# Shifting the upper words of float64 weights: shift and AND with a constant column instead of two shifts by scalars

## The chip, the cores and the metric

The kernel runs on one core of one Trainium2 chip. The metric is the device time of one execution in microseconds; the kernel before takes 724.04 us (median of 3 runs, 724.02 to 725.27).

## What is computed

Causal attention with a gate bias for 2 x 8 heads of 576 positions, then two feed-forward blocks on its 1152 rows of 512 numbers. The first mixes four experts, the second multiplies two projections. The change lies in the loading of the second block's weights, which arrive as float64.

```python
out = np.zeros((N, D), dtype=np.float32)
for e in range(E):                       # E = 4, D = 512, F = 1024
    h = np.maximum(x @ w1[e], 0.0)
    out += p[:, e:e + 1] * (h @ w2[e])
...
a = x @ w_a                              # 512 -> 1536, float64 weights
b = x @ w_b
return (a * b @ w_out).astype(np.float32)
```

## The kernel before

Every float32 product is three TensorE products of a high and a low part (`mm3`, line 281: high by high, high by low, low by high). A weight is therefore split when it has landed: ScalarE writes the high part `wh` (line 80 or 225), and GpSimd or VectorE writes the low part `wl` (line 81 or 227) as the weight minus `wh`.

Attention and the plain part of the first block come first. From about 200 us on the kernel is a stream of units, each a pair of 256 weight columns against all rows: `quadrants` (line 417) forms the first-layer products `psq` and `pst` by a scheme of seven block products whose sums VectorE makes (line 436), and second-layer units add a tile of 128 rows into `acc` (lines 335 and 1225). `ab_stage(m)`, m = 0 to 5, is one pair of the second block: products with `wa`, products with `wb`, their product split by VectorE into `h2h` and `h2l` (lines 1202, 80, 81), and products with `wo`.

The float64 weights come as pairs of 32-bit words, in loads of 512 KB, into three SBUF buffers named `raw` (line 155; the DMA, line 156, is issued by SP). `narrow` (line 159) makes a float32 from each pair: ScalarE takes the absolute value of the upper word read as a float (line 161), GpSimd clamps it (line 162), VectorE shifts it (line 166), VectorE ORs in the lower word shifted right by 29 (line 170), and VectorE ORs in the sign and top exponent bit of the upper word (line 174). Line 174 is the last to read `raw`. A unit has six such pieces of 128 x 512 numbers: two for `wa`, two for `wb` (tile `tp`, followed on GpSimd by the four sums of lines 189 to 192 and two splits of 128 x 1024) and two for `wo` (tile `t`, followed by a split of 128 x 512). Six units make 36 pieces, so 36 instructions of each of the lines 161, 162, 166, 170 and 174; they run from 424 to 683 us.

The order on each engine is not written out: the program is recorded in the order of `run` (line 1309), where `weight_step` (line 251) loads or splits one piece per 3 us of planned TensorE work, and a scheduler then orders each engine's instructions by its own estimate of their durations. An instruction whose estimate changes can therefore move others. Engines run their queues strictly in order and wait on semaphores.

Of the kernel before, what the change touches and what calls it, by code (L numbers as in the profile page):

```python
# [8 lines left out]
F32 = mybir.dt.float32  # L9
F32R = mybir.dt.float32r  # L10
BF16 = mybir.dt.bfloat16
I32 = mybir.dt.int32
AF = mybir.ActivationFunctionType
ALU = mybir.AluOpType
# [6 lines left out]
P = 128  # L21
# [38 lines left out]
def fused_kernel(ctx, tc, qk0, v0, qT, kT, v, s, dp, w1, w2, wa, wb, wo, out):  # L60
    nc = tc.nc

    const = ctx.enter_context(tc.tile_pool(name="const", bufs=1))
# [9 lines left out]
    pr = const.tile([P, NTT, E], F32, name="pr")  # L73
    den = const.tile([P, NTT], F32, name="den")
    ident = const.tile([P, P], F32, name="ident")

    ckD = dram.tile([3, len(GROUPS), H, S], F32, name="ckD")

# [4 lines left out]
    def open_pools(c, names):  # L83
        for name, bufs in names:
            pools[name] = c.enter_context(tc.tile_pool(name=name, bufs=bufs))
# [72 lines left out]

    def narrow(t, lo, hi):

        nc.scalar.activation(out=t.bitcast(F32), in_=hi.bitcast(F32), func=AF.Abs)  # L161
        nc.gpsimd.tensor_scalar(  # L162
            out=t.bitcast(F32), in0=t.bitcast(F32), scalar1=2.0**-15, scalar2=GMAX,
            op0=ALU.max, op1=ALU.min,
        )
        nc.vector.tensor_scalar(
            out=t, in0=t, scalar1=5, scalar2=2,
            op0=ALU.logical_shift_left, op1=ALU.logical_shift_right,
        )
        nc.vector.scalar_tensor_tensor(  # L170
            out=t, in0=lo, scalar=29, in1=t,
            op0=ALU.logical_shift_right, op1=ALU.bitwise_or,
        )
        nc.vector.scalar_tensor_tensor(  # L174
            out=t, in0=hi, scalar=-(1 << 30), in1=t,
            op0=ALU.bitwise_and, op1=ALU.bitwise_or,
        )
# [21 lines left out]
    def split_piece(r, key, form, wide, src, j):  # L199
        wh, wl = slabs[key]  # L200
        if form == "half" and wide:
            t = pools["cv"].tile([P, SL], I32, tag="t", name="t")
            narrow(t, r[:, :, 0], r[:, :, 1])
            split(wh[:, j, :], wl[:, j, :], t.bitcast(F32), nc.gpsimd)
        elif form == "half":
            split(wh, wl, r, nc.gpsimd)
        elif form == "pair" and wide:
            if j == 0:
                wides[key] = pools["cv"].tile([P, NC, 2 * P], I32, tag="tp", name="tp")
            t = wides[key]  # L210
            narrow(t[:, 2 * j : 2 * j + 2], r[:, :, :, 0], r[:, :, :, 1])
            if j:
                split_pair(key, t.bitcast(F32), nc.gpsimd)
        elif form == "pair":
            split_pair(key, r, nc.vector)
        else:
            nsplit[0] += 1
            lo_eng = nc.gpsimd if nsplit[0] % 2 or nsplit[0] <= NFIRST else nc.vector
            two = slice(2 * j, 2 * j + 2)
            if nsplit[0] <= NFIRST:  # L220
                nc.gpsimd.tensor_scalar(
                    out=wh[:, two, :], in0=r, scalar1=1.0, scalar2=1.0, op0=ALU.mult, op1=ALU.mult
                )
            else:
                nc.scalar.activation(out=wh[:, two, :], in_=r, func=AF.Copy)
            for m in (2 * j, 2 * j + 1):
                lo_eng.tensor_tensor(
                    out=wl[:, m, :], in0=r[:, m - 2 * j, :], in1=wh[:, m, :].bitcast(F32), op=ALU.subtract
                )
# [530 lines left out]
    for base in (0, -32, -64, -96):  # L760
        nc.gpsimd.affine_select(
            out=sel_, in_=sel_, pattern=[[-1, H]], compare_op=ALU.not_equal,
# [5 lines left out]
        out=causal[:, S - P :], in_=causal[:, S - P :], pattern=[[-1, P]], compare_op=ALU.is_ge, fill=MASKED,  # L768
# [6 lines left out]
        out=cum[:NS, :NT0], data0=ones[:NS, :NT0], data1=sc[:, :NT0], initial=0.0,  # L775
        op0=ALU.mult, op1=ALU.add,
    )
    in_order(nc.vector.tensor_scalar(
        out=cb, in0=cum[:NS, :NT0], scalar1=1.0, scalar2=1.0, op0=ALU.mult, op1=ALU.mult
    ))  # L780
    for lo_, eng in ((slice(32, NB), nc.vector), (slice(96, NS), nc.gpsimd)):
        in_order(eng.tensor_tensor(
            out=cb[lo_], in0=cum[lo_, :NT0], in1=cb[lo_].bitcast(F32), op=ALU.subtract
# [197 lines left out]
    def close_attention():  # L981
        actx.close()
        open_pools(ctx, [("h2", 2), ("raw", 3), ("q", 2), ("cv", 1)])
        pools["late"] = True
        late_ps.append(ctx.enter_context(tc.tile_pool(name="ps_m2", bufs=5, space=PSUM)))
        for part_ in ("h", "l"):
            tq[part_] = ctx.enter_context(tc.tile_pool(name="tq" + part_, bufs=1)).tile(
                [P, 3, 2, SL], F32R, name="tq" + part_
            )
# [336 lines left out]
    mixed.clear()  # L1326
    passed.clear()
    close_attention()
    run(after, False)

# [59 lines left out]
```

## Time and profile before

| what | value |
|---|---|
| median of 3 runs | 724.04 us |
| profiled execution | 725.65 us, span 723.90 us (1.75 us lie around the span) |
| TensorE busy | 98% of the span, granted clock 10 tenths of full speed throughout |
| VectorE, GpSimd, ScalarE busy | 71%, 55%, 45% |
| costliest group | line 281, 334 products each of `wh,h2h`, `wl,h2h` and `wh,h2l`, 392, 389 and 390 ns |

TensorE's products overlap in the trace, so its busy time says only that some product was under way. What an instruction of another engine costs is read from the stretch it lies in: here 424 to 683 us, where the float64 weights are converted.

### The profile page before, as it was taken

What the parts mean: (1) busy time and instruction counts of PE and PEld (TensorE: products, weight loads), DVE (VectorE), ACT (ScalarE), POOL (GpSimd) and SP (SyncE); (2) the same over time, 40 slices, a digit from 0 to 9 for tenths busy, and PEclk for the clock granted to TensorE, in tenths of its full rate; (3) what the DMA queues carried; (4) which work ended last, traced back from release to release, by engine and by line L of the source; (5) the groups of instructions that cost most, each with busy time, mean ns of one, the idle gap of its engine ahead of it and who ended that gap; (6) DMA issues with size and microseconds to landing.
All of it is one profiled execution on the core that took longest, in us unless ns stands there. A gap on an engine that the chain in (4) does not pass through costs nothing.

```text
span 723.9 us, 10979 instructions
## 1 busy us (share of the span) xinstructions
PE 710.9 (98%) x3884; PEld 620.9 (86%) x3886; DVE 512.9 (71%) x1060; ACT 323.5 (45%) x722; POOL 398.8 (55%) x329
## 2 busy tenths in 40 slices
PE   9999999999999999999999999999999999999998
PEld 5886798999899888888888888887999888888886
DVE  5586878767686866765655666589973969787674
ACT  3597899877434333331223123334544424243410
POOL 5476866655235544430333057687277879788600
PEclk9999999999999999999999999999999999999999
DMA  8665434442111211120111021222021222212003
GB/s 328 209 176 141 126 88 119 124 120 62 57 41 58 89 58 58 59 65 24 58 59 47 13 88 59 88 87 88 30 87 59 88 88 83 92 60 88 1 0 131
DMA packets 33724, 61.42 MB, mean 85 GB/s; under 512 B 3285, under 2 KB 17525, under 8 KB 33669
## 3 DMA queue, kind: packets, MB, share of 16 engines
q1 hardware_dynamic: 33189, 59.61, 26.6%
q10 hardware_dynamic: 480, 1.11, 0.4%
q8 instruction: 31, 0.51, 0.3%
q14 instruction: 24, 0.20, 0.1%
HBM read 55.11 MB, written 2.58 MB: 80 GB/s over the span
## 4 chain that ended last, share of the span: by engine, by line
PE 76%; DVE 9%; POOL 5%; issue 4%; ACT 4%; DMA 3%; SPq 0%; POOLq 0%; ACTq 0%; DVEq 0%
PE ps L281 34%; PE psq L281 24%; PE pst L281 6%; PE av L702 2%; PE tr L670 2%; POOL wl L81 2%; PE ps L1037 2%; DMA raw<-in_wo 1%; DVE el L686 1%; DVE tp L174 1%; PE lullps L736 1%; ACT e L651 1%; DVE h2l L81 1%; DVE tp L170 1%; POOL tp L162 1%
## 5 line engine op out<-in xcount | busy, mean ns | idle before, releaser
L281 PE MATMUL ps<-wh,h2h 128*128 128x512 f32 (+1 forms) x334 | 131.1, 392 | 0.6 <-ACT h2h L80 0.6
L281 PE MATMUL ps<-wl,h2h 128*128 128x512 f32 (+1 forms) x334 | 129.9, 389 | 0.0
L81 POOL TENSOR_TENSOR wl<-raw,wh 128x1024 fp32r<-128x1024 f32 x24 | 58.2, 2433 | 129.0 <-ACT wh L80 98.6
L281 PE MATMUL ps<-wh,h2l 128*128 128x512 f32 (+1 forms) x334 | 125.6, 390 | 0.0
L335 DVE SCALAR_TENSOR_TENSOR acc<-ps,pr,acc 128x512 f32<-128x512 f32 x111 | 82.3, 746 | 41.1 <-PE ps L281 40.4
L281 PE MATMUL psq<-xh,wh 128*128 128x448 f32 (+1 forms) x224 | 81.7, 365 | 0.1
L281 PE MATMUL psq<-xh,wl 128*128 128x448 f32 (+1 forms) x224 | 81.4, 363 | 0.0
L281 PE MATMUL psq<-xl,wh 128*128 128x448 f32 (+1 forms) x224 | 81.3, 363 | 0.0
L281 PEld LDWEIGHTS ps<-wh,h2l 128*128 128x128 f32 x334 | 62.7, 188 | 13.2
L281 PEld LDWEIGHTS ps<-wh,h2h 128*128 128x128 f32 x334 | 62.8, 188 | 13.0 <-ACT h2h L80 1.3
L346 ACT ACTIVATE h2h<-psq 128x448 fp32r<-128x448 f32 (+1 forms) x56 | 29.5, 530 | 95.5 <-PE psq L281 76.4
L281 PEld LDWEIGHTS ps<-wl,h2h 128*128 128x128 f32 x334 | 62.8, 188 | 10.9
L81 POOL TENSOR_TENSOR wl<-sums,wh 128x1024 fp32r<-128x1024 f32 x24 | 58.3, 2427 | 4.9 <-ACT wh L80 4.9
L80 ACT ACTIVATE wh<-raw 128x1024 fp32r<-128x1024 f32 x24 | 25.5, 1062 | 69.6 <-PE ps L281 53.0
L281 PE MATMUL psq<-tqh,wh 128*128 128x448 f32 x144 | 53.0, 368 | 1.3 <-DVE h2l L81 0.9
L281 PE MATMUL psq<-tql,wh 128*128 128x448 f32 x144 | 52.6, 365 | 0.0
L281 PE MATMUL psq<-tqh,wl 128*128 128x448 f32 x144 | 52.5, 364 | 0.0
L162 POOL TENSOR_SCALAR tp<-tp 128x512 f32<-128x512 f32 x24 | 48.0, 2017 | 5.8 <-ACT tp L161 5.8
L686 DVE TENSOR_TENSOR el<-tr,eh 128x512 fp32r<-128x512 f32 (+5 forms) x80 | 38.3, 484 | 16.4 <-ACT eh L685 15.6
L659 POOL TENSOR_SCALAR e<-e,r 128x448 f32<-128x448 f32 (+4 forms) x64 | 37.8, 595 | 17.5 <-DVE r L658 12.9
L281 PEld LDWEIGHTS psq<-xh,wh 128*128 128x128 f32 x224 | 42.1, 188 | 4.3 <-ACT s L445 0.9
L281 PEld LDWEIGHTS psq<-xl,wh 128*128 128x128 f32 x224 | 42.1, 188 | 3.5
(205 smaller groups left out, 1877.2 us busy)
## 6 DMA issues: line engine op xcount, KB each, us to landing
raw<-in_w SPq DMA_DIRECT2D x32, 512.0 KB
raw<-in_wa SPq DMA_DIRECT2D x12, 512.0 KB
raw<-in_wb SPq DMA_DIRECT2D x12, 512.0 KB
raw<-in_wo SPq DMA_DIRECT2D x12, 512.0 KB
kr<-in_kT SPq DMA_DIRECT2D x16, 288.0 KB
w<-in_w SPq DMA_DIRECT2D x8, 512.0 KB
vr<-in_v SPq DMA_DIRECT2D x16, 160.0 KB
kb<-ks SPq DMA_DIRECT2D x16, 144.0 KB
```

The costliest lines, as they stand in the source:

```text
L80: nc.scalar.activation(out=hi, in_=src, func=AF.Copy)
L81: lo_eng.tensor_tensor(out=lo, in0=src, in1=hi.bitcast(F32), op=ALU.subtract)
L162: nc.gpsimd.tensor_scalar(out=t.bitcast(F32), in0=t.bitcast(F32), scalar1=2.0**-15, scalar2=GMAX, op0=ALU.max, op1=ALU.min,)
L170: nc.vector.scalar_tensor_tensor(out=t, in0=lo, scalar=29, in1=t, op0=ALU.logical_shift_right, op1=ALU.bitwise_or,)
L281: ins = nc.tensor.matmul(ps, lhsT=l, rhs=r, start=first and k == 0, stop=last and k == 2, skip_group_check=more)
L335: nc.vector.scalar_tensor_tensor(out=dst, in0=ps, scalar=share, in1=dst, op0=ALU.mult, op1=ALU.add)
L346: nc.scalar.activation(out=hh, in_=src, func=AF.Relu)
L659: nc.gpsimd.tensor_scalar(out=t.e, in0=t.e, scalar1=r, scalar2=1.0, op0=ALU.mult, op1=ALU.mult)
L670: ins = nc.tensor.transpose(ps[:, c - c0, :], t.e[:, k0 : k0 + P], ident)
L686: nc.vector.tensor_tensor(out=j.el[:, c0:c1, x], in0=src, in1=hi.bitcast(F32), op=ALU.subtract)
L702: ins = nc.tensor.matmul(ps[:, o:], lhsT=j.vs[:, c, :], rhs=e[:, c, o:], start=(m == 0), stop=(m == len(mms) - 1),)
L1037: ins = nc.tensor.matmul(ps, lhsT=w, rhs=x, start=start, stop=stop)
```

## The change

The shift left by 5 and right by 2 (which clears the two top bits and leaves the word shifted left by 3) becomes a shift left by 3 and an AND with a mask of 30 ones. The mask is one 32-bit word per partition (`low30`, filled once by GpSimd with the float whose bits are 0x3FFFFFFF), read by every element through a step of zero. The VectorE instruction is then a `scalar_tensor_tensor`, of the kind of lines 170 and 174, instead of a `tensor_scalar`.

```diff
@@ fused_kernel
     ident = const.tile([P, P], F32, name="ident")
+    low30 = const.tile([P, 1], F32, name="low30")
@@ narrow
+        mask = low30.bitcast(I32)
+        mask = mask.broadcast_to(t.shape) if len(t.shape) == 2 else mask.unsqueeze(2).broadcast_to(t.shape)
         nc.scalar.activation(out=t.bitcast(F32), in_=hi.bitcast(F32), func=AF.Abs)
...
-        nc.vector.tensor_scalar(
-            out=t, in0=t, scalar1=5, scalar2=2,
-            op0=ALU.logical_shift_left, op1=ALU.logical_shift_right,
+        nc.vector.scalar_tensor_tensor(
+            out=t, in0=t, scalar=3, in1=mask,
+            op0=ALU.logical_shift_left, op1=ALU.bitwise_and,
         )
@@ close_attention
         pools["late"] = True
+        nc.gpsimd.memset(low30, 2.0 - 2.0**-23)
```

Line numbers of the changed kernel are 1 to 4 higher; its lines 164, 165, 169, 173 and 177 are the old 161, 162, 166, 170 and 174. SP's queue of DMAs keeps its order. The memset stands among the first rows of GpSimd's queue, at the start of the program. From the first shift on, the scheduler has put some instructions of the other four engines elsewhere; the numbers of products stay.

VectorE, the fourth unit of the second block, first half of `wo` (the shift of `t`; `pst` and `psq` are first-layer products). Before:

```order
L1202 TENSOR_TENSOR pst<-pst,sr 128x512
L1202 TENSOR_TENSOR psq<-psq,u_6208 128x448
L166 TENSOR_SCALAR t<-t 128x512
L81 TENSOR_TENSOR h2l<-pst,h2h 128x2x256
L170 SCALAR_TENSOR_TENSOR t<-raw,t 128x512
L81 TENSOR_TENSOR h2l<-psq,h2h 128x448
L174 SCALAR_TENSOR_TENSOR t<-raw,t 128x512
```

and in the changed kernel:

```order
L1206 TENSOR_TENSOR psq<-psq,u_6210 128x448
L82 TENSOR_TENSOR h2l<-pst,h2h 128x2x256
L1206 TENSOR_TENSOR psq<-psq,s_6208 128x448
L82 TENSOR_TENSOR h2l<-psq,h2h 128x448 x2
L439 TENSOR_TENSOR psq<-psq,u_6412 128x448
L169 SCALAR_TENSOR_TENSOR t<-t,low_72 128x512
L1206 TENSOR_TENSOR psq<-psq,u_6209 128x448
L439 TENSOR_TENSOR u_6536<-psq,s_6535 128x448
L173 SCALAR_TENSOR_TENSOR t<-raw,t 128x512
L82 TENSOR_TENSOR h2l<-psq,h2h 128x448
L177 SCALAR_TENSOR_TENSOR t<-raw,t 128x512
```

The shift has gone from ahead of the three low parts `h2l` of the unit to behind them.

VectorE, a little earlier, the two pieces of the `wb` weights of that unit (tile `tp`). Before:

```order
L166 TENSOR_SCALAR tp<-tp 128x512
L1225 TENSOR_TENSOR acc<-ps_6325,acc 128x512
L170 SCALAR_TENSOR_TENSOR tp<-raw,tp 128x512
L1225 TENSOR_TENSOR acc<-ps_6333,acc 128x512
L174 SCALAR_TENSOR_TENSOR tp<-raw,tp 128x512
L166 TENSOR_SCALAR tp<-tp 128x512
L1225 TENSOR_TENSOR acc<-ps_6341,acc 128x512
```

and in the changed kernel:

```order
L169 SCALAR_TENSOR_TENSOR tp<-tp,low_72 128x512
L1229 TENSOR_TENSOR acc<-ps_6335,acc 128x512
L173 SCALAR_TENSOR_TENSOR tp<-raw,tp 128x512
L1229 TENSOR_TENSOR acc<-ps_6343,acc 128x512
L169 SCALAR_TENSOR_TENSOR tp<-tp,low_72 128x512
L177 SCALAR_TENSOR_TENSOR tp<-raw,tp 128x512
```

The shift of the second piece has moved ahead of the first piece's last instruction, the one that frees its `raw`.

## Rows read from the trace of the kernel before

**Rows 1.** The page's busy time, share of the span and instructions of each engine.

```profile
PE 710.9 (98%) x3884; PEld 620.9 (86%) x3886; DVE 512.9 (71%) x1060; ACT 323.5 (45%) x722; POOL 398.8 (55%) x329
```

**Rows 2.** Busy time by stretch: us; PE, PEld, DVE, ACT, POOL; clock, DMA.

```profile
530.00:580.00 50.00, 50.00 (x268) 44.92 (x267) 35.65 (x55) 22.43 (x37) 41.73 (x28) 1.00 0.24 74
580.00:630.00 50.00, 49.46 (x257) 43.46 (x256) 39.47 (x63) 16.68 (x26) 39.90 (x26) 1.00 0.26 81
630.00:680.00 50.00, 48.54 (x251) 42.20 (x251) 38.53 (x65) 19.73 (x31) 44.26 (x28) 1.00 0.21 67
```

**Rows 3.** PE's waits from 424 to 724 us: total, times, longest.

```profile
PE psq L281 <- DVE h2l L81: 0.9, 3, 0.5
PE ps L281 <- ACT h2h L80: 0.6, 1, 0.6
```

**Rows 4.** The chain that ended last, 400 to 724 us: start, us, what.

```profile
581.29 3.67 POOL wl L81 x2
...
605.58 0.42 DVE tp L166
...
665.13 0.75 DVE tp L166
...
676.35 3.92 PE psq L281 x18
```

**Rows 5.** Instructions of a line: ns minimum, median, maximum; line 166 from 530 to 680 us.

```profile
L166 DVE TENSOR_SCALAR tp<-tp x16: 409/420/825, 535.0 to 665.1; 128x512 int32<-128x512 int32 x16
L166 DVE TENSOR_SCALAR t<-t x8: 411/806/1700, 562.9 to 679.4; 128x512 int32<-128x512 int32 x8
...
L170 DVE SCALAR_TENSOR_TENSOR tp<-raw,tp x24: 674/682/1116, 427.2 to 665.9; 128x512 int32<-128x512 int32 x24
```

**Rows 6.** Who waited for line 174 (us, times).

```profile
  ACT wh L80: 49.4, 19
```

**Rows 7.** Timeline, line 174 on VectorE and SP's loads: start, us.

```profile
427.88 0.69 DVE L174 SCALAR_TENSOR_TENSOR tp<-raw,tp 128x512 int32<-128x512 int32 x1
...
664.45 0.68 DVE L174 SCALAR_TENSOR_TENSOR tp<-raw,tp 128x512 int32<-128x512 int32 x1
...
428.63 0.37 SPq L156 DMA_DIRECT2D raw<-in_wa  x1
...
665.20 0.34 SPq L156 DMA_DIRECT2D raw<-in_wo  x1
```

**Rows 8.** Timeline, low halves of `wo` on GpSimd and TensorE's first products with them.

```profile
525.34 1.30 POOL L81 TENSOR_TENSOR wl<-t,wh 128x512 fp32r<-128x512 f32 x1 [3.07 <-ACT wh L80]
...
581.29 1.30 POOL L81 TENSOR_TENSOR wl<-t,wh 128x512 fp32r<-128x512 f32 x1 [1.29 <-ACT wh L80]
...
534.74 0.39 PE L281 MATMUL ps<-wl,h2h 128*128 128x512 f32 x1
...
583.51 0.39 PE L281 MATMUL ps<-wl,h2h 128*128 128x512 f32 x1
```

**Rows 9.** Timeline, GpSimd's splits and VectorE's shift and OR beside them.

```profile
576.26 2.59 POOL L81 TENSOR_TENSOR wl<-tp,wh 128x1024 fp32r<-128x1024 f32 x1
...
599.45 2.40 POOL L81 TENSOR_TENSOR wl<-sums,wh 128x1024 fp32r<-128x1024 f32 x1
...
577.10 2.30 DVE L170 SCALAR_TENSOR_TENSOR t<-raw,t 128x512 int32<-128x512 int32 x1
...
600.50 1.64 DVE L166 TENSOR_SCALAR t<-t 128x512 int32<-128x512 int32 x1
602.06 0.68 DVE L81 TENSOR_TENSOR h2l<-pst,h2h 128x512 fp32r<-128x512 f32 x1
...
638.24 1.42 DVE L166 TENSOR_SCALAR t<-t 128x512 int32<-128x512 int32 x1
```

**Rows 10.** A GpSimd memset at the start; the one VectorE instruction with a step of zero.

```profile
2.19 0.09 POOL L867 MEMSET pick<- 32x4 f32 x1
...
L851 DVE TENSOR_TENSOR xq<-av,r x4: 424/425/425, 16.5 to 27.7; 128x256 f32<-128x256 f32 x4
```

## The prediction

> **What bounds the kernel now.** I began with the busy shares: TensorE works in 98% of the span, VectorE in 71%, GpSimd in 55% [rows 1]. That reads as a kernel bound by TensorE, in which a VectorE instruction is free. A share over the whole span cannot say so for one stretch, so I next took the stretch in which all 36 changed instructions lie, and its later part in steps of 50 us. TensorE is busy for 50.00 us of the first 50, then 49.46, then 48.54 [rows 2]: its idle time appears only where VectorE (35.65, 39.47, 38.53) and GpSimd (41.73, 39.90, 44.26) are both near 80%. The two depend on each other piece by piece, so two engines at 80% are a full pair.
>
> The waits of TensorE name what was late: the low part `h2l` from VectorE and the high part `h2h` from ScalarE [rows 3]. The chain of work that ended last says the same in order of time. From 581.29 to 676.35 us it leaves TensorE altogether and runs through the conversion of the weights and the queues of the three other engines, and only then returns to TensorE's products [rows 4]. Over those 95 us, time added to the conversion has no TensorE work on the chain to hide behind.
>
> Two more views show that the conversion is a closed loop. ScalarE waited 49.4 us in 19 places for line 174, VectorE's last instruction of a `tp` or `t` piece [rows 6]. And the loads wait for it too: of the 35 loads issued after 424 us, 33 were issued within 0.1 us of the end of a line 174, since that frees one of the three `raw` buffers. The first is 427.88 + 0.69 = 428.57, issue at 428.63, the last 664.45 + 0.68 = 665.13, issue at 665.20 [rows 7]. What a piece loses on VectorE, the next pieces get later.
>
> **The change part by part.** *The 36 shifts.* An undisturbed shift takes 0.42 us (median of the 16 of `tp`). The new instruction has the shape, type and kind of line 170, two tensors of 128 x 512 whole numbers in SBUF, whose median is 682 ns [rows 5]. So each costs 0.68 - 0.42 = 0.26 us more, 36 x 0.26 = 9.4 us in all.
>
> The Trainium skill (VectorE: DVE Perf Modes, the section "The perf-mode tier table") speaks against the change in the same sense: instructions with one source in SBUF reach twice the rate for 32-bit elements, those with two sources do not. From its clock of 0.96 GHz I estimate 512 / 0.96 / 2 = 267 ns a shift; the two medians differ by 262 ns and agree.
>
> *How much of it lies on the path.* Take the lead of the weights over TensorE. The `wo` half that GpSimd finished at 525.34 + 1.30 = 526.64 is first used at 534.74, 8.1 us later; that of 581.29 + 1.30 = 582.59 at 583.51, 0.9 us later [rows 8]. The first 12 shifts, before 530 us, delay the loop by 12 x 0.26 = 3.1 us, less than the 8.1 us of lead, so I take nothing for them: the cover is TensorE's other products, and if the lead were used up they would cost those 3.1 us. Behind it lie 16 + 8 = 24 shifts [rows 5]. The last, at 679.4 us, belongs to the last `wo` half, after which no load follows; I leave it out. 23 x 0.26 = 6.0 us. The bounds are far apart: only four shifts stand on the chain by name, the first at 605.58 and the last at 665.13 us [rows 4], which gives 1.0 us, and all 36 on the path give 9.4. I take 6.0, because the loop makes each shift delay the next load, whether or not the chain happens to name it.
>
> *The wait beside GpSimd.* Where GpSimd is in a split, VectorE's conversion waits for it, in the old form and in that of line 170. The split that ends at 576.26 + 2.59 = 578.85 holds a line 170 until 577.10 + 2.30 = 579.40, 0.55 us after it. The one that ends at 599.45 + 2.40 = 601.85 holds a shift until 600.50 + 1.64 = 602.14, 0.29 us after it [rows 9]. The difference is the same 0.26, already counted, provided the shift meets GpSimd at the same moment. It need not: the order changes. The shift at 600.50 came when the split was 1.05 us old and waited about 1.64 - 0.42 = 1.2 us; it can come at once and wait 2.4. Three of the eight shifts of `t` after 530 us are of this sort, at 1.64 and 1.42 [rows 9] and up to 1.70 [rows 5], so the bounds are 3 x 1.2 = 3.6 us more on top, or 3.6 us of waiting gone. On TensorE's side such a wait showed as up to 0.5 us of idle time [rows 3], since the `h2l` at 602.06 was queued behind the shift [rows 9]. In the new order the shift stands behind those `h2l`, which removes that, while the wait itself can grow; I take zero and keep the ends.
>
> *The rest of the order.* SP's queue is unchanged. In the `tp` pairs the second shift now stands ahead of the first piece's line 174, so that piece's `raw` comes free up to 0.68 us later, and the second piece's sooner; together zero, with 12 pairs x 0.68 = 8.2 us as an upper bound that needs every pair to be late for it. TensorE's products change places among themselves with the same count; zero, as long as their operands are there.
>
> *The memset* is one more small row at the start, about 0.09 us on GpSimd [rows 10]; zero, and 0.1 at most. The tile adds four bytes a partition.
>
> **The sum** is +6.0 us. The profiled execution took 725.65 us, of which 723.90 are its span; with the change it would take 731.7. The median of the runs is 1.61 us lower, 724.04, so the forecast for the median is **730.0 us**. I expect TensorE's granted clock to stay at its upper level of 2.4 GHz, as in all three stretches of rows 2.
>
> **The rivals.** *Hidden after all.* TensorE is the busiest engine and its idle time from 530 to 680 us is only 0.54 + 1.46 = 2.0 us [rows 2]; VectorE has some 11 of every 50 us free, and 24 x 0.26 = 6.2 us would fit in. Then the median stays at 724.0. Against it: the free time is time spent waiting for GpSimd, not time in which a piece can run.
>
> *Faster: the column is no second stream.* The shift would take 0.68 us but never wait for GpSimd, nor make GpSimd wait. The place is the `t` shift of 600.50 and its two like: there 1.64 us becomes 0.68, the `h2l` behind it comes about 1 us earlier, and the idle time of TensorE goes, at most the 2.0 us of rows 2: 724.0 - 2.0 = **722.0**. It decides if a shift that starts in the middle of a split ends 0.68 us after its start. For it: no row shows a column with step zero, both inputs in SBUF, beside GpSimd; the one instruction with such a column (line 851) has its other input in PSUM and stays within 424 to 425 ns [rows 10]. Against it: the mask is passed as a tensor, and line 170 with two tensors does wait.
>
> The Trainium skill (SBUF — State Buffer, the section "SBUF: two separate sides") bears on this rival: an instruction of VectorE with two SBUF inputs contends with a GpSimd instruction that reads SBUF for one pair of ports, which the first to come holds alone. By that rule the column makes the shift wait, and the sum stays at 6.0 instead of this rival's -2.0. The 2.30 us of line 170 agree; for a step of zero no row here shows it.
>
> *Worse.* All 36 shifts on the path and three longer waits: 9.4 + 3.6 = 13.0, **737.0**. For it: the order puts more of VectorE's work in front of the instructions that free `raw`. Against it: the lead of 8.1 us before 530 us.
>
> **How the numbers follow.** The forecast (3 to 9.5 us slower) gets 0.66, the worse case 0.13, hidden 0.13, the faster case 0.08. A measurement of this kernel can tell about 0.2%, 1.4 us. Faster by more than that is the faster case alone, 0.08; within it the hidden case, 0.13; slower 0.66 + 0.13 = 0.79. The range runs from the hidden case's middle, 724.0, to 733.5, the sum with all 36 shifts on the path; it leaves out the faster case, half of the hidden one and half of the worse one, 0.08 + 0.06 + 0.06 = 0.20.
>
> **What would show it.** Right: the line of the shift at a median near 0.68 us for 36 instructions, with a few over 2 us beside a split; the line 177 of the last piece ending 6 to 9 us later than the 683 us of before; TensorE's idle time between 530 and 690 us grown from 2 to about 8 us; loads still issued at the end of that line. Wrong: a shift in the middle of a split at 0.68 us (the faster case); the last piece later but TensorE without new idle time (hidden); or an undisturbed shift near 0.42 us, which would take the whole term away.

## The result and the profile after

| what | before | after |
|---|---|---|
| median on the same chip | 725.27 us (5 runs, 724.02 to 725.50) | 736.15 us (5 runs, 733.92 to 737.93) |
| ratio, 95% interval | | 1.0149 [1.0130, 1.0167] |
| profiled execution | 725.65 us, span 723.90 | 736.15 us, span 734.4 |

The change makes the kernel slower by 10.8 us (9.4 to 12.1 by the interval). The prediction had the direction and a part of the mechanism, +6.0 us and 730.0; the time lies outside its range, which ended at 733.5. Of that distance 1.2 us are the kernel before, which took 725.27 us here and 724.04 where the forecast started; but the 10.8 us alone are more than the range's 9.5. Below, "us by the ratio" is always the ratio's excess times 725 us. In e1, e3, e4, e5, e9 and e10 one or two runs took well longer than the others, at a lower granted clock: the ratios leave these out, the medians below do not, and of the two profiles taken in such a run (e3 and e10) only lengths and starts of single VectorE and GpSimd instructions are read.

The page's busy time after, the same columns as [rows 1]:

```profile
PE 713.2 (97%) x3884; PEld 623.4 (85%) x3886; DVE 529.0 (72%) x1060; ACT 324.0 (44%) x722; POOL 398.3 (54%) x330
```

VectorE is busy for 16.1 us more, although the 36 longer instructions account for 36 x 0.26 = 9.4. The three conversion lines together went from 80.3 to 96.2 us, so the rest, too, lies in them: instructions that are longer than when undisturbed, as the one at 568.11 us below. The page shows no more than that; the stretches do (columns as in [rows 2]; the first two stretches lie ahead of them):

```profile
424.00:500.00 76.00, 75.38 (x384) 65.09 (x383) 57.44 (x89) 24.99 (x39) 50.60 (x32) 1.00 0.22 70
500.00:530.00 30.00, 29.04 (x167) 25.88 (x167) 25.60 (x44) 15.53 (x31) 9.08 (x8) 1.00 0.16 53
530.00:580.00 50.00, 47.17 (x249) 41.99 (x248) 37.97 (x53) 23.26 (x38) 39.20 (x24) 1.00 0.20 64
580.00:630.00 50.00, 49.67 (x258) 44.00 (x257) 44.02 (x64) 17.08 (x26) 39.62 (x28) 1.00 0.29 90
630.00:680.00 50.00, 47.07 (x249) 41.20 (x248) 38.87 (x60) 15.77 (x27) 39.87 (x26) 1.00 0.24 80
680.00:734.40 54.40, 48.61 (x243) 42.22 (x242) 35.67 (x56) 10.42 (x18) 12.07 (x8) 0.97 0.12 44
```

From 530 to 680 us TensorE idles for 2.83 + 0.33 + 2.93 = 6.1 us, where it idled for 2.0 in [rows 2]. It also idles for 0.62 + 0.96 = 1.6 us ahead of 530 us, where the prediction expected nothing, and the last stretch has a mean clock of 0.97. Who made TensorE wait from 530 to 690 us (total, times, longest), to be read beside [rows 3]:

```profile
PE psq L284 <- DVE h2l L82: 5.2, 4, 1.6
PE psq L284 <- DVE psq L439: 1.2, 1, 1.2
PE psq L284 <- DVE u L439: 0.8, 1, 0.8
PE ps L284 <- DVE h2l L82: 0.7, 1, 0.7
...
```

It is VectorE nearly every time, and `h2l` above all: 0.9 us before, 5.9 us now. These are not the conversion's instructions but those queued behind them. VectorE's timeline ahead of two of these waits:

```profile
533.23 2.36 DVE L173 SCALAR_TENSOR_TENSOR t<-raw,t 128x512 int32<-128x512 int32 x1
535.51 0.61 DVE L82 TENSOR_TENSOR h2l<-psq,h2h 128x448 fp32r<-128x448 f32 x1
...
682.36 2.33 DVE L177 SCALAR_TENSOR_TENSOR t<-raw,t 128x512 int32<-128x512 int32 x1
684.61 0.68 DVE L82 TENSOR_TENSOR h2l<-pst,h2h 128x512 fp32r<-128x512 f32 x1
```

TensorE goes on at 536.18 and 685.44 us, after 1.25 and 1.45 us. Two more of the waits for `h2l` (1.57 and 0.75 us, to 573.13 and 651.80) end behind the shifts at 568.11 and 647.38, of 2.88 and 2.70 us. So 5.0 of the 5.9 us come behind a conversion instruction that was itself held up by some 1.7 to 2.2 us. The shift itself (line 169, ns minimum/median/maximum):

```profile
L169 DVE SCALAR_TENSOR_TENSOR tp<-tp,low x24: 675/682/1535, 425.9 to 675.9; 128x512 int32<-128x512 int32 x24
L169 DVE SCALAR_TENSOR_TENSOR t<-t,low x12: 675/686/2879, 478.8 to 692.4; 128x512 int32<-128x512 int32 x12
```

and the last line 177 in VectorE's timeline, which is the end of the last piece:

```profile
695.20 0.68 DVE L177 SCALAR_TENSOR_TENSOR t<-raw,t 128x512 int32<-128x512 int32 x1
```

The undisturbed shift takes 0.68 us instead of the 0.42 of [rows 5], as the prediction said. The last piece ends at 695.88 instead of 683.18 us, 12.7 us later. One of the shifts beside a split, in the timeline of GpSimd and VectorE:

```profile
566.16 1.91 POOL L165 TENSOR_SCALAR t<-t 128x512 f32<-128x512 f32 x1
568.05 2.40 POOL L82 TENSOR_TENSOR wl<-sums,wh 128x1024 fp32r<-128x1024 f32 x1
...
568.11 2.88 DVE L169 SCALAR_TENSOR_TENSOR t<-t,low 128x512 int32<-128x512 int32 x1 [1.04 <-POOL t L165]
```

The clamp releases the shift and the split in the same moment; the split is 0.06 us ahead, and the shift ends at 570.99, 0.54 us after the split's 570.45. So a column with a step of zero does count as a second stream here: the new shift waits beside GpSimd as line 170 did at 577.10 in [rows 9], which ended 0.55 us after its split.

### The profile page after: what moved, and what is told of

It is laid out like the page before. It is cut to its first block, busy times and chain, and to the rows that moved or that the text cites. A ratio compares the mean times of both kernels' runs of the same rounds, so it can differ in the third digit from the quotient of the medians.

```text
span 734.4 us, 10975 instructions
## 1 busy us (share of the span) xinstructions
PE 713.2 (97%) x3884; PEld 623.4 (85%) x3886; DVE 529.0 (72%) x1060; ACT 324.0 (44%) x722; POOL 398.3 (54%) x330
## 4 chain that ended last, share of the span: by engine, by line
PE 76%; DVE 10%; POOL 5%; ACT 4%; issue 3%; DMA 2%; SPq 0%; POOLq 0%; DVEq 0%; ACTq 0%
PE ps L284 34%; PE psq L284 24%; PE pst L284 6%; PE av L705 2%; PE tr L673 2%; POOL wl L82 2%; PE ps L1041 2%; DVE t L169 1%; DVE el L689 1%; DVE tp L177 1%; DVE tp L173 1%; ACT e L654 1%; PE lullps L739 1%; PE sc L631 1%; PE sc L630 1%
## 5 line engine op out<-in xcount | busy, mean ns | idle before, releaser
L284 PE MATMUL pst<-xh,wl 128*128 128x256 f32 x160 | 45.2, 282 | 0.0
```

The source lines that it names most:

```text
L284: ins = nc.tensor.matmul(ps, lhsT=l, rhs=r, start=first and k == 0, stop=last and k == 2, skip_group_check=more)
```

## The experiments

The scheduler reorders the program when an instruction's estimate changes, so form and order of the change come mixed. In the kernels below the order is held: a table names each engine's instructions in the wanted order, and between neighbours stands an edge that fixes the order of issue and lets nobody wait for a result. No run holds the order of before and changes nothing else, so what the edges themselves cost is not measured; e10 and e11, which are held and faster than the kernel before, speak against much.

```diff
-    run(after, False)
+    run(after, False); in_given_order(tc, aside)
...
+        for a, b in zip(row, row[1:]):      # row: one engine's instructions, by the table
+            tc.add_manual_dep(b, a.name, nosync, reason="given order")
```

| run | shift | order | median us | before us | ratio, 95% interval | us by the ratio |
|---|---|---|---|---|---|---|
| e1 | new | before | 733.69 | 724.38 | 1.0122 [1.0108, 1.0137] | +8.8 |
| e2 | old | changed | 728.94 | 724.38 | 1.0068 [1.0052, 1.0084] | +4.9 |
| e3 | old, and 0.272 us of memset | before | 733.47 | 724.38 | 1.0123 [1.0108, 1.0138] | +8.9 |
| e4 | first 12 new | before | 728.24 | 724.38 | 1.0044 [1.0031, 1.0057] | +3.2 |
| e5 | new | before, one exchange | 732.31 | 725.16 | 1.0096 [1.0082, 1.0110] | +7.0 |
| e6 | last 24 new | before | 731.95 | 725.16 | 1.0086 [1.0068, 1.0104] | +6.2 |
| e7 | old | TensorE's of changed | 733.06 | 725.16 | 1.0111 [1.0094, 1.0129] | +8.0 |
| e8 | old, and 0.165 us of memset | before | 730.38 | 725.16 | 1.0077 [1.0065, 1.0089] | +5.6 |
| e9 | old | changed, ScalarE mended | 730.20 | 725.32 | 1.0052 [1.0029, 1.0074] | +3.8 |
| e10 | old, one column of 512 (two of a `tp` piece) | before | 721.40 | 725.32 | 0.9936 [0.9911, 0.9961] | -4.6 |
| e11 | old | before, three exchanges | 723.66 | 725.32 | 0.9970 [0.9949, 0.9992] | -2.2 |
| e12 | new | before, three exchanges | 733.79 | 725.32 | 1.0100 [1.0061, 1.0138] | +7.3 |

### Form or order (e1, e2)

e1 is the changed kernel with the table of before; e2 is the kernel before with the table of the changed one.

> The new shift and the memset, with every engine's instructions held in the order of the kernel before; nothing but the form of the 36 shifts differs. Length on the loop (the sum of the prediction): 23 x 0.26 us, 725.3 + 6.0 = about 731. Order (the rival theory that the moved instructions carry most of it): within 2 us of before, 724 to 727. Wait beside GpSimd in addition to length: nearly all of the +10.9 us, less what TensorE's lower clock took, 732 to 735, with several shifts of t over 2 us beside a split.

> The old shift, with every engine's instructions held in the order of the changed kernel (without the memset); nothing but the order differs from before. Order theory: most of the +10.9 us, 731 to 736. Length theory, and wait beside GpSimd: 725 to 727, since in this order every shift is as short as it was.

The form alone costs 8.8 us, more than the prediction's 6.0 and nearly all of 36 x 0.26 = 9.4. The order alone costs 4.9 with the old shift. The two do not add up (13.7 against 10.8): beside the long shift the new order adds only some 2 us, and the intervals of e1 and of the changed kernel overlap. Where e2's time goes, TensorE's waits from 424 us on:

```profile
PE psq L281 <- DVE h2l L81: 2.4, 2, 1.5
PE psq L281 <- ACT sc L1157: 1.0, 1, 1.0
PE ps L281 <- DVE h2l L81: 0.5, 1, 0.5
...
```

### Length without the port (e3, e8)

Is it the length, or the second stream? e3 gives VectorE the same length of other work, which reads no SBUF; e8 about half of it.

```diff
-        nc.vector.tensor_scalar(
+        shift = nc.vector.tensor_scalar(
             out=t, in0=t, scalar1=5, scalar2=2,
             op0=ALU.logical_shift_left, op1=ALU.logical_shift_right,
         )
+        fill = nc.vector.memset(pad, 1.0).ins     # 256 columns; in e8 pad[:, :128]
```

> The old shift in the order of before, and right behind each of the 36 a memset of 256 two-byte columns of a tile that nobody reads; by the memset of 576 columns at 538 ns it is estimated at 0.24 us, about the 0.26 us that the new shift is longer. Nothing else differs. Length theory: VectorE is kept as long per piece as by the new shift, so as much as the new shift in the same order, about +6, 731. Wait beside GpSimd: the memset reads no SBUF and holds nothing that GpSimd wants, so clearly less than the new shift in the old order, 0 to +4, 725 to 729.

> As e3_old_plus_fill, with 128 columns instead of 256 in each memset, about 0.14 instead of 0.272 us. Length theory, in proportion: half of the +9.1 us, 728.5 to 729.5. Lost turns at the ports: by steps, since a piece is late enough to lose a turn or is not; near nothing (under 727) or nearly all (over 731).

The memsets, in e3 and in e8:

```profile
L172 DVE MEMSET pad<- x36: 272/272/272, 438.2 to 699.4; 128x256 bf16 x36
```

```profile
L172 DVE MEMSET pad<- x36: 165/165/165, 425.1 to 685.2; 128x128 bf16 x36
```

All 36 of each run are equally long, so a memset never waits for GpSimd. 36 x 0.272 = 9.8 us of it cost 8.9, 36 x 0.165 = 5.9 us cost 5.6, and the new shift's 9.4 cost 8.8: some 0.93 us per us, whatever VectorE does in it. In the order of before, then, the wait of the shift itself does not come on top of its length. e8's median, 730.38 us, lies outside both expected ranges; its memset was longer than expected (0.165 instead of 0.14 us), and in proportion to that length e3's 8.9 gives 5.4. As a sum the step theory falls, within the interval of 4.7 to 6.5. In one place it holds: the longest of TensorE's waits in e8 is as long as in e1 and e4,

```profile
PE ps L286 <- DVE acc L340: 1.8, 1, 1.8
```

and the section on 482 us shows where it comes from.

### The two halves of the term (e4, e6)

`done` counts the pieces in the order in which the program makes them; the 12 that run before 530 us are the first ten, the 13th and the 14th. Against the changed kernel:

```diff
+        done[0] += 1
+        if done[0] <= 10 or done[0] in (13, 14):      # e4; in e6 "if not (...)"
+            nc.vector.scalar_tensor_tensor(
+                out=t, in0=t, scalar=3, in1=mask,
...
+        else:
+            nc.vector.tensor_scalar(
+                out=t, in0=t, scalar1=5, scalar2=2,
...
```

> The order of before; the new shift in the 12 that run before 530 us, the old one in the 24 behind. The prediction's cover (8.1 us of lead): no change, 724 to 726. If the lead is no cover for the loop: at least 12 x 0.26 = 3.1 us, about 728.4, and in windows TensorE's idle time between 500 and 580 us grows.

> The order of before; the old shift in the 12 that run before 530 us, the new one in the 24 behind: the complement of e4_first12, and the very kernel for which the prediction's sum holds. Prediction: 23 x 0.26 = +6.0 us, 730.4. If the two parts add up to e1 (9.1 us at a median of 733.7, of which e4 took 3.9): +5.2, 729.6. If wait beside GpSimd doubles the length behind 530 us: +9 and more, 733.

e6 is the prediction's sum as a kernel, and it holds: +6.2 us (4.9 to 7.5) against +6.0. That they agree to 0.2 us is luck: its six runs lie in two groups, 729.04 and 729.19, and 731.70 to 732.61 us, and its profile is of the first. e4 is the part that the sum took as covered, and there it fails: +3.2 us (2.2 to 4.1) against zero; 12 x 0.26 is 3.1. The two add up to 9.4, e1 measured 8.8. TensorE's waits from 424 us on add up in the same way. First e4, then e6, then e1:

```profile
PE ps L292 <- DVE acc L346: 1.8, 1, 1.8
PE psq L292 <- DVE h2l L83: 0.9, 3, 0.6
PE psq L292 <- DVE u L447: 0.4, 1, 0.4
...
```

```profile
PE psq L292 <- DVE u L447: 2.7, 3, 1.0
PE psq L292 <- DVE h2l L83: 2.3, 3, 1.1
...
```

```profile
PE psq L284 <- DVE u L439: 2.7, 3, 1.0
PE psq L284 <- DVE h2l L82: 2.3, 3, 1.1
PE ps L284 <- DVE acc L338: 1.8, 1, 1.8
...
```

`h2l` and `u` in e4 stand at 0.9 and 0.4, as in the kernel before; its whole addition is one wait for `acc`, a sum that VectorE takes out of PSUM. So the 3.2 us are not twelve delays of 0.26. Behind the wait, which ends at 483.66 us, the granted clock falls from 1.00 to 0.50:

```profile
485.00:486.00 1.00, 1.00 (x4) 0.77 (x3) 1.00 (x3) 1.00 (x2) 0.25 (x1) 0.50 0.00 0
```

From 484 to 488 us it is 0.75, 0.50, 0.50 and 0.54, which I estimate at 1.7 us of lost time. The one run of e4 at a mean clock of 1.000 took 726.32 us, those at 0.998 took 727.61 to 728.34. One run is little, and e8's runs do not sort this way (730.65 us at 1.000, 730.29 to 730.98 at 0.998), so how much of the 3.2 us is the wait and how much the clock stays open. The weights, whose lead of 8.1 us the prediction had measured, are not in the list: they did come in time.

### What waits near 482 us (e5)

The timeline there, VectorE and GpSimd in the kernel before:

```profile
480.33 0.68 DVE L170 SCALAR_TENSOR_TENSOR t<-raw,t 128x512 int32<-128x512 int32 x1
480.93 0.74 DVE L335 SCALAR_TENSOR_TENSOR acc<-ps,pr,acc 128x512 f32<-128x512 f32 x1
...
480.29 2.98 POOL L81 TENSOR_TENSOR wl<-tp,wh 128x1024 fp32r<-128x1024 f32 x1
```

and in e1:

```profile
480.49 2.88 DVE L173 SCALAR_TENSOR_TENSOR t<-raw,t 128x512 int32<-128x512 int32 x1
483.30 0.74 DVE L338 SCALAR_TENSOR_TENSOR acc<-ps,pr,acc 128x512 f32<-128x512 f32 x1
...
480.44 2.38 POOL L82 TENSOR_TENSOR wl<-tp,wh 128x1024 fp32r<-128x1024 f32 x1
```

The two engines meet at one port within 0.05 us. In the kernel before VectorE's OR gets it, and GpSimd's split takes 2.98 instead of 2.38 us: 0.6 us, and on GpSimd. In e1 the split gets it, the OR takes 2.88 instead of 0.68 us, and the `acc` behind it, for which TensorE waits, is 2.4 us later. I call that a lost turn. It is not the shift that pays but the OR after it. The same OR loses its turn in e4 (2.88 us), in e12 (2.89) and in e8, where half of the added time is enough for all of it (GpSimd and VectorE):

```profile
479.92 2.40 POOL L83 TENSOR_TENSOR wl<-tp,wh 128x1024 fp32r<-128x1024 f32 x1
...
479.96 2.90 DVE L175 SCALAR_TENSOR_TENSOR t<-raw,t 128x512 int32<-128x512 int32 x1
```

e5 exchanges the OR with the `acc` ahead of it:

```diff
 L350 h2l<-psq,h2h
 L439 psq<-psq,s
+L173 t<-raw,t
 L338 acc<-ps,pr,acc
-L173 t<-raw,t
 L338 acc<-ps,pr,acc
```

> The new shift in the order of before, as in e1_new_old_order, and one exchange of two neighbours in VectorE's order: the OR of line 173 for the first t piece stands ahead of the evacuation acc of line 338 that preceded it, so that it starts about 0.66 us sooner, ahead of GpSimd's split at 480.44 us instead of 0.05 us behind it. Lost turn at the ports (theory formed from e1): the OR takes 0.7 instead of 2.88 us, TensorE's wait of 1.8 us near 482 us goes, and the run falls from 733.7 by about 2 us to 731 to 732. Length alone: 36 shifts are as long as before, 733 to 734.

```profile
479.71 1.21 DVE L173 SCALAR_TENSOR_TENSOR t<-raw,t 128x512 int32<-128x512 int32 x1
480.84 1.40 DVE L338 SCALAR_TENSOR_TENSOR acc<-ps,pr,acc 128x512 f32<-128x512 f32 x2
```

The OR keeps its turn (1.21 us; the 0.5 on top lies beside one of the short `sums`), and the cost by the ratio falls from 8.8 to 7.0 us, the way that was expected; the median, 732.31, is 0.3 us above the expected range. TensorE's wait for `acc` only went from 1.8 to 1.2 us and did not go, as expected, to zero, and the two intervals overlap (e1 7.8 to 9.9, e5 5.9 to 8.0). That a lost turn takes part in the first 12 shifts' cost is seen; how much of it is the turn's is not settled. Nor do lost turns alone make the cost: of conversion instructions of 2 us and more e1 has six, e3, e8 and e12 three each, the kernel before two, and e3 and e12 cost as much as e1 within their intervals.

### Where the order costs (e7, e9)

> The old shift; TensorE's instructions in the order of the changed kernel, all other engines in the order of before. If the order's cost in e2_old_new_order (+4.6 us) is TensorE's, because a product stands too early there: 728 to 730, with the wait of 1.1 us near 505 us that e2 and the changed kernel show. If it is VectorE's and ScalarE's: 724 to 726.

e7 lies outside both expectations and answers the question badly. TensorE's order alone, without the moves of the others that belong to it, costs 8.0 us, more than the whole of e2, and in waits that e2 does not have (6.1 us in 3 times for `u`); the wait near 505 us is not among them. The moves of the four engines belong together, and a mixture says nothing of their parts.

e9 mends one place. In e2's trace ScalarE's `sc` and `wh` stand behind two copies that wait 3.6 us:

```profile
504.99 0.98 ACT L1165 ACTIVATE u<-psq 128x448 f32<-128x448 f32 x2 [3.63 <-PE psq L1142]
505.85 0.55 ACT L1157 ACTIVATE sc<-psq 128x448 f32<-128x448 f32 x1
506.28 0.64 ACT L80 ACTIVATE wh<-t 128x512 fp32r<-128x512 f32 x1
```

```diff
 L1157 s<-psq
+L1157 sc<-psq
+L80 wh<-t
 L1165 u<-psq
 L1165 u<-psq
-L1157 sc<-psq
-L80 wh<-t
```

> As e2_old_new_order (the old shift in the order of the changed kernel), with one exchange on ScalarE: the copy sc of line 1157 and the high part wh<-t of line 80 stand ahead of the two copies u of line 1165, which wait 3.6 us for TensorE near 505 us. Theory formed from e2's trace: these two waits in the queue are the start of the order's cost; TensorE's wait of 1.0 us near 505 us goes, the piece t is split some 5 us sooner, and 728.9 falls to 726 to 727.5. Rival: the cost of the order arises later, behind 530 us, on VectorE; then 728 to 729, the wait near 505 gone all the same.

The wait near 505 us goes, but the waits for `h2l` further on grow from 2.4 us to 3.7:

```profile
PE psq L281 <- DVE h2l L81: 3.7, 4, 1.4
...
```

e2 and e9 cannot be told apart (+4.9 and +3.8 us, intervals 3.8 to 6.1 and 2.1 to 5.4). The rival fits, though e9's median lies above both expected ranges: without the wait near 505 us the order costs as much, and the waits left are nearly all for VectorE, behind 530 us. e2's longest, 1.46 us to 678.77, has an `h2l` behind a lost turn, as in the changed kernel:

```profile
675.68 2.34 DVE L174 SCALAR_TENSOR_TENSOR t<-raw,t 128x512 int32<-128x512 int32 x1
677.94 0.68 DVE L81 TENSOR_TENSOR h2l<-pst,h2h 128x512 fp32r<-128x512 f32 x1
```

That these turns are the whole cost of the order no run shows.

### Below and beside the kernel before (e10, e11, e12)

```diff
-            out=t, in0=t, scalar1=5, scalar2=2,
+            out=t[..., :1], in0=t[..., :1], scalar1=5, scalar2=2,
```

> The order of before; each of the 36 old shifts shifts the first of its 512 columns only (the other 511 columns stay unshifted, so this part of the computation is left out), which shortens it from 0.42 to some 0.1 us. If the time goes with the length of VectorE's part as it did upwards (8.9 us for 36 x 0.272 = 9.8 us added): -0.9 x 36 x 0.3 = -9.7 us, 715. If the kernel before is bound by TensorE and only the way up costs: no less than the 5 us in which TensorE is idle behind 424 us, 719 to 722.

The shift takes some 0.15 us and the kernel changes by -4.6 us (-6.5 to -2.8). That is near the 5 us of TensorE's idle time that the expectation names, and half of what the slope of the way up would give. Up, a microsecond of VectorE's time costs 0.93; down, it gives back half of that. That the gain stops because TensorE has no more idle time to lose fits the size; no trace here shows it.

e11 and e12 use the time of a lost turn. VectorE's order is exchanged in three places (near 563, 600 and 638 us), so that work from PSUM runs while GpSimd holds the port:

```diff
 L1202 psq<-psq,u
-L166 t<-t
 L81 h2l<-pst,h2h
-L170 t<-raw,t
 L81 h2l<-psq,h2h
+L166 t<-t
+L170 t<-raw,t
 L174 t<-raw,t
```

> The old shift and the order of before, with one exchange in three places of VectorE's order (near 563, 600 and 638 us): the two low parts h2l, which read PSUM, stand ahead of the shift of t, which waits 1.0 to 1.3 us for GpSimd's split there. Nothing is left out. Lost turns at the ports: VectorE works on h2l while the split runs, TensorE's waits of 0.6 us near 602 and 0.4 near 640 go, the piece ends about 1 us sooner each time: 721.5 to 723.5, faster than before. Length alone: the same work in the same queue, 724 to 725.

> As e11_old_fill_turn with the new shift. Lost turns: of the 8.9 us of e1_new_old_order some 2 to 3 go, 730.5 to 732. Length alone: as e1, 733 to 734.

e11's timeline, the place that [rows 9] show at 600.50:

```profile
598.90 0.69 DVE L81 TENSOR_TENSOR h2l<-pst,h2h 128x512 fp32r<-128x512 f32 x1
599.51 0.61 DVE L81 TENSOR_TENSOR h2l<-psq,h2h 128x448 fp32r<-128x448 f32 x1
600.04 0.81 DVE L166 TENSOR_SCALAR t<-t 128x512 int32<-128x512 int32 x1
```

The shift takes 0.81 instead of 1.64 us. TensorE's waits for `h2l`, 0.9 us in [rows 3], are gone from the list, and the median is 723.66 us against 725.32: faster by 2.2 us (0.6 to 3.7). It beats both kernels, with the old shift and nothing left out. How much, the two traces put lower: from the first shift to the end they take 297.6 us before and 296.4 in e11, 1.2 us less; the other 1.5 us between their spans lie ahead of the first shift, where both do the same. With the new shift the same exchanges give +7.3 us (4.4 to 10.0), not to be told from e1. In e1 the shifts near 565, 604 and 643 us take 2.20, 2.25 and 2.23 us; in e12 none takes 2 us, and the cost is not clearly lower.

## Why the prediction was half right

**Right: the length and its place.** Each shift costs 0.26 us more (0.68 against 0.42), and from 530 us on the sum is right: 6.0 predicted for 23, 6.2 measured for 24 (e6). TensorE's idle time from 530 to 690 us grew from 2 us to 6.1 + 2.7 = 8.8, about the 8 that were named, and 33 loads are still issued within 0.1 us of the end of line 177. One of the signs failed: the last line 177 ends 12.7 us later, where 6 to 9 were named.

**Wrong, and the largest step: "the first 12 shifts ... less than the 8.1 us of lead, so I take nothing".** They cost 3.2 us (e4). The lead was real but was the lead of the weights over TensorE, one of two things that VectorE owes TensorE. The other, taking the sums out of PSUM, stands in the same queue behind the conversion and had less: in e1 and e4 one `acc` is late by more than its lead, and TensorE waits 1.8 us for it. The upper end of that term, 3.1 us, meets the 3.2 by chance, since twelve delays of 0.26 are not what e4's trace shows, but one lost turn and a stretch of low clock behind it.

**Too small: "I take 6.0", between 1.0 and 9.4.** All 36 x 0.26 = 9.4 us is close to the 8.8 of e1, so the upper bound was nearer than the sum, with the same reserve for the first 12. Whether the last shift costs nothing no run tells: 23 and 24 shifts differ by 0.26 us, far inside e6's interval.

**Wrong: "I expect TensorE's granted clock to stay at its upper level".** In windows of 1 us it falls to 0.50, the level of 1.2 GHz:

```profile
684.00:685.00 1.00, 0.00 (x0) 0.00 (x0) 1.00 (x2) 0.28 (x1) 1.00 (x2) 0.98 0.00 0
685.00:686.00 1.00, 0.56 (x2) 0.55 (x3) 1.00 (x3) 0.49 (x2) 0.84 (x2) 0.50 0.00 0
686.00:687.00 1.00, 1.00 (x4) 0.91 (x3) 0.97 (x3) 0.95 (x3) 0.71 (x1) 0.50 0.00 0
...
688.00:689.00 1.00, 1.00 (x6) 0.90 (x5) 0.97 (x3) 0.94 (x2) 0.97 (x1) 0.81 0.00 0
```

TensorE had stood still for 1.22 and then 1.45 us, waiting for VectorE's `psq` and `h2l`; a product of 448 columns then takes 0.57 us instead of 0.37, until 688.2. The five runs sort by it: 733.92 and 734.23 us at a mean clock of 1.000, 736.15 at 0.998, 737.66 and 737.93 at 0.995. e1 has 732.49 and 733.12 us at 1.000. So at full clock the changed kernel is some 1.3 us above e1, 0.9 of which is the difference of the runs of before that stood beside them (725.27 and 724.38), and the rest of the distance of the medians goes with the clock. This sorts runs of one kernel; no run here takes the clock alone away.

**The rest of the order, taken as zero,** was wrong for the old shift (+4.9 us, e2) and small beside the long one, as just said.

**The wait beside GpSimd, "I take zero and keep the ends",** held as a sum in the order of before and failed as a picture. Three shifts of `t` take 2.88, 2.79 and 2.70 us against the 1.70, 1.64 and 1.42 of before, 3.6 us more, of which 2.8 are waiting and 0.8 their length. The lines of the OR wait longer too, which the term did not price: 2.88 us at 480.49 in e1, 2.33 at 682.36 in the changed kernel, each with a wait of TensorE behind it. But e3, whose memsets wait for nobody, costs as much as the new shift, and its OR at 493.33 us takes 2.88 as well: there the turn is lost because a piece is late, and the old shift is enough for that. Whether the changed kernel, with its other order, would cost less without these waits no run shows.

**The rivals.** *Faster: no second stream* is refuted by the 2.88 us at 568.11. The Trainium skill (SBUF — State Buffer, the section "SBUF: two separate sides") says that a VectorE instruction with two SBUF inputs contends with a GpSimd instruction that reads SBUF for a pair of ports; the trace agrees, with that 2.88 us, also for an input of step zero. *Hidden* is refuted by e3: 8.9 of 9.8 us come out. *Worse* gave 737.0 with a chance of 0.13 and came nearest to the 736.15 measured: both its parts, 9.4 us of length and 3.6 of longer waits, are near to what e1 and the three shifts show in size. They do not add up as it had it: e3 has the cost without longer shifts, and 9.4 + 3.6 = 13.0 lies above the interval of 9.4 to 12.1.

## What to carry to other kernels

A lead belongs to one product of an engine: before calling an added instruction covered, look at everything that the same queue owes to the bottleneck (here the sums in PSUM, not the weights), and take the least lead. With two engines both near 80% busy, this kernel paid for added time nearly one for one and got about half back for time removed. Where one engine is held up beside another, as the shift beside GpSimd's split, look for work in its queue that is not held up and put it first: here three exchanges in the order made the kernel faster by 2.2 us (0.6 to 3.7).

## What was not expected of the hardware

- Who gets the port cannot be read from starts 0.04 us apart, and the two outcomes differ in price: recorded 0.04 us behind the split, the OR took 0.68 us in the kernel before (and the split 0.6 us more) but 2.90 us in e8; at 0.05 us behind, in e1, it took 2.88.
- Beside GpSimd's clamp VectorE was held up for only a part of the clamp's span. Two clamps fill 632.25 to 636.06 us; a shift of `tp` that starts at 634.22, with the second, takes 1.09 us, 0.41 more than alone, where beside a split a shift takes up to 2.88.
- The same wait of TensorE did not always cost the same. In e1, e4, e8 and e12 it stood for 1.8 us near 483 us, waiting for `acc`. In e12 the granted clock is 0.50 from 485 to 488 us, in e4 and e8 it falls to 0.50 as well, in e1 it stays at 1.00. What decides that is open.
